# When batch 3 is folded: its copies, sending, addition and stage one in other units

## The chip, the cores and the metric

The kernel runs on one core of one Trainium2 chip. The metric is the time of one execution on the device, in microseconds; the time of a version is the median of its runs. Matrix products run on TensorE (PE in the profile), elementwise work on VectorE (DVE), ScalarE (ACT) and GpSimd (POOL). SyncE (SP) issues most of the DMA transfers; GpSimd issues some too, from its own queue.

## The reference

```python
X = np.fft.fft(x, axis=1)             # x: (8, 3072, 256), float32
X = np.fft.fft(X, axis=2)
t = X.real.astype(np.float32).reshape(24576, 256)
h = np.maximum(np.maximum(t @ w1, t @ w2), t @ w3)    # three matrices 256 x 768
out = (h @ w_out).astype(np.float32)                  # 768 x 256
```

So each of the 8 batches is mixed by a Fourier transform over 3072 rows and 256 columns, of which the real part is kept, and each of the resulting 24576 rows then goes through a layer whose hidden value is the largest of three products.

## The kernel before, in words

**What is computed where.** The transform over the 256 columns is folded into the weights once, at the start (`gE`, `gO`, `gD`, `gw`). The transform over the 3072 rows is done per batch by the class `Mix`, in two stages: seven pieces of *stage one* (`s0` to `s6`, L546), whose results ACT copies to `z_all`, and six pieces of *stage two* (`k0` to `k5`, L570 and L572, and a small `end`), whose results ACT copies to the batch's tile `t`, an even part `tE` and an odd part `tO`. Output rows come in pairs, row r and its mirror image, from even plus odd and even minus odd.

**The units.** A batch's second half, the layer, is cut into three blocks of 512 columns and six chunks of the hidden dimension: 18 units per batch. A unit makes the hidden values of its chunk for the plus rows (`unit_plus`, L590 and L591) and, one unit later, for the minus rows (`unit_minus`, L598); ACT (L604) and DVE (L605) take the largest of the three. Between them PE works off a queue of output products (`l2_block`, L615, 12 for each of four slots per block). A slot's output also needs the linear part: `l2_even` (L628, copied to `even` by ACT) and `l2_odd`, a product of the odd part into the same bank `po` (L639), of which DVE makes `other` (L642) and POOL the second half of the line `even` (L645). DVE then adds the line to `po` and gives `ot` (L665). There are two `po` banks, so the L639 of a slot waits for the L665 of the slot two before it. The plus rows of `ot` are stored by SP (L678), the minus rows by POOL with an indirect DMA (L668, the scatter; 128 KB). There are six `ot` buffers.

**Folding a batch.** While the units of batch b run, the input of later batches is made ready. For batches 2 to 7, the *folded* ones, it goes like this:

- `fetch` loads four chunks of the batch's rows, fp32, to four buffers `xs` (`load_chunk`: four DMAs of 198 or 192 KB per chunk on SP's queue, L111, and five small ones for the last chunk, L123).
- `turn_part` makes POOL copies. A *mirrored* one (L177) puts half of a chunk, turned round and in bf16, to the one tile `xb`; every second one is followed by a small copy (L181). A *natural* one (L172) puts half of a chunk to the batch's tile `xw`. There are eight of each per batch. A chunk's buffer `xs` is free for the next load when its mirrored and natural copies are done.
- `send_turned` sends `xb` to memory (`held`) with eight DMAs of 96 KB on SP's queue (L190).
- `add_turned` adds `held` to `xw` with two accumulating DMAs of 384 KB on POOL's queue (L199).
- Stage one of the batch reads `xw`.

**Who decides the order.** The order of every engine's instructions is written out by the program: `at(b, unit, fn)` puts a step behind the unit `unit` of batch b (a unit of 18 or more is one of the batch after it), and the main loop runs the steps planned for a unit when it has issued that unit. Each engine works its own instructions in this order, and one that waits holds up what is queued behind it on the same engine, DMA issues on SP's and POOL's queues among them.

During batch b, batch b + 1 goes through stage one and two (`begin`, and `steady`, units 8 to 20 in 13 steps), batch b + 2 is copied, sent and added, and the chunks of batch b + 3 are loaded (L852 to L869). Before the change, the folded batches have one plan, except that the one folded during batch 0, batch 2, has a later one.

Of the kernel before, what the change touches and what calls it, by code (L numbers as in the profile page):

```python
# [33 lines left out]
def kernel(  # L34
# [127 lines left out]
    def turn_part(b, ch, part):  # L162

        xs = raw[b, ch]
        if b not in turned:
            xw = xw_pool.tile([96, 34 * 128], BF16, name="xw", tag="xw")
            turned[b] = xw.rearrange("p (dl bb) -> p dl bb", bb=128)
        v = turned[b]
        half, natural = part % 2, part // 2
        if natural:  # L170
            d0, d1 = ((0, 17), (17, 33))[half]
            nc.gpsimd.tensor_copy(v[:, d0:d1, ch * 32:ch * 32 + 32],  # L172
                                  xs[:, 0:32 * 64].rearrange("p (bb dl) -> p dl bb", dl=64)[:, d0:d1, :])
            return
        c0 = 96 - 32 * ch
        d0, d1 = ((0, 16), (16, 32))[half]
        nc.gpsimd.tensor_copy(mir[:, d0:d1, c0:c0 + 32],  # L177
                              bass.AP(xs.tensor, xs.offset + 33 * 64 - 1 - d0,
                                      [xs.ap[0], [-1, d1 - d0], [-64, 32]]))
        if half:  # L180
            nc.gpsimd.tensor_copy(v[:, 33, c0:c0 + 32],  # L181
                                  bass.AP(xs.tensor, xs.offset + 32 * 64, [xs.ap[0], [-64, 32]]))
# [3 lines left out]
    def send_turned(b):  # L186

        hd = turn_pool.tile([8, 12 * 4096], BF16, name="held", tag="held")
        for i in range(8):
            nc.sync.dma_start(out=hd[7 - i].rearrange("(a r) -> a r", a=12),  # L190
                              in_=xb[i * 12:(i + 1) * 12])
        held[b] = hd

    def add_turned(b):

        hd = held[b]
        v = turned[b]
        for c in range(2):
            nc.gpsimd.dma_start(out=v[:, 1 + 16 * c:17 + 16 * c, :].rearrange("p dl bb -> p (dl bb)"),  # L199
                                in_=bass.AP(hd.tensor, hd.offset + 11 * 4096 + 2048 * c,  # L200
                                            [[12 * 4096, 8], [-4096, 12], [1, 2048]]),
                                accum_op=ALU.add)
# [608 lines left out]
    def at(b, unit, fn):  # L811
        plan.setdefault((b + unit // UNITS, unit % UNITS), []).append(fn)

    def piece(b, what):
        mm = mix(b)
        if what[0] == "s":
            mm.s(int(what[1:]), turned[b])
        elif what[0] == "k":
            mm.k(int(what[1]))
        else:  # L820
            mm.end()

    def fetch(b, ch):
        raw[b, ch] = load_chunk(b, ch)
# [2 lines left out]
             ("k0",), ("k1",), ("k2",), ("k3",), ("k4",), ("k5", "end"))  # L827
    begin = {0: (11, 12, 13, 13, 14, 14, 15, 16, 16, 17, 18, 19, 20),
             1: (11, 12, 12, 13, 13, 14, 14, 15, 16, 17, 18, 19, 20),
             B - 2: (8, 8, 9, 9, 10, 11, 11, 12, 13, 14, 15, 16, 17)}  # L830
    steady = tuple(range(8, 21))

# [19 lines left out]
    for b in range(B - 1):  # L852
        for i, whats in enumerate(ahead):
            for what in whats:
                at(b, begin.get(b, steady)[i], lambda b=b, what=what: piece(b + 1, what))
        if b + 2 < B:
            mirrored, natural, send_at, add_at = (
                (range(4, 12), range(12, 20), 13, 19) if b else
                ((11, 11, 12, 13, 14, 15, 16, 17), (12, 14, 16, 18, 19, 19, 20, 21), 18, 21))
            for i in range(8):  # L860
                at(b, mirrored[i], lambda b=b, i=i: turn_part(b + 2, i // 2, i % 2))
            at(b, send_at, lambda b=b: send_turned(b + 2))
            for i in range(8):
                at(b, natural[i], lambda b=b, i=i: turn_part(b + 2, i // 2, 2 + i % 2))
            at(b, add_at, lambda b=b: add_turned(b + 2))
            if b + 3 < B:
                for ch in range(4):
                    at(b, (14, 16, 18, 20)[ch] if b else (18, 19, 21, 23)[ch],
                       lambda b=b, ch=ch: fetch(b + 3, ch))  # L869

    for b in range(B):
# [77 lines left out]
```

## Time and profile before

| | |
|---|---|
| median of 3 runs | 416.75 us (414.35 to 416.84) |
| the profiled execution's own time | 415.72 us |
| span of the profile, first to last instruction | 413.6 us |
| mean granted TensorE clock | 0.990 |
| PE busy | 390.9 us, 95% of the span |
| POOL busy | 333.5 us, 81% |
| DVE busy | 309.4 us, 75% |
| ACT busy | 266.0 us, 64% |
| L668, scatter on POOL, 92 | 103.4 us, 1124 ns each |
| L645, `even` on POOL, 92 | 70.3 us, 764 ns each |
| L177, mirrored copies, 48 | 51.3 us, 1070 ns each |
| L172, natural copies, 48 | 53.0 us, 1106 ns each |
| DMA | 62.12 MB, mean 150 GB/s; 114929 of 134758 packets under 512 B |

Busy time is the time in which an engine had an instruction under way. PE's starts are exact, its ends are modelled, so a PE that is busy all the time is at its peak only if its clock is full. The profile's slices cut the span in 40 pieces of 10.3 us; a digit is the busy share in tenths. The clock of PE is a share too: 1.00 is full speed. An issue of a DMA on SP's queue that lasts long is one that SP could not hand over; when the data has landed is in the completion records of the trace, per transfer.

### The profile page before, as it was taken

To read this page: it belongs to the slowest core of one execution; us is meant where nothing else is said; L and a number is where in the kernel's file an instruction comes from. 1 tells how busy PE (TensorE), PEld (TensorE's weight loads), DVE (VectorE), ACT (ScalarE), POOL (GpSimd) and SP (SyncE) were. 2 spreads that over 40 slices of the span, in tenths; PEclk is the share of its full clock that TensorE was granted. 3 is DMA by queue.
4 is the path that set the end of the run, shared out by engine and by line. 5 is a ranking of instruction groups with operands and counts; after the bars stand their busy time and mean duration, and the time that the engine had idled before them with its cause. 6 is when DMAs were issued, how large, how long until landed. Compare 5 with 4: busy or idle time off the path is not lost.

```text
span 413.6 us, 8843 instructions
## 1 busy us (share of the span) xinstructions
PE 390.9 (95%) x2880; PEld 261.6 (63%) x2880; DVE 309.4 (75%) x556; ACT 266.0 (64%) x489; POOL 333.5 (81%) x458
## 2 busy tenths in 40 slices
PE   0999999996599999999999999999999999999996
PEld 0465677763367666666666666766667666766665
DVE  8898766784467877768876877778777777778883
ACT  6787767664176667665776577666776676655550
POOL 9599989993889999998999898998999744446641
PEclk9999999999699999999999999999999999999999
DMA  9999894487758874698477965788552722212214
GB/s 116 190 196 184 185 216 130 117 179 145 197 152 214 175 177 144 178 197 180 128 197 191 187 163 149 200 184 183 161 142 76 133 74 78 78 51 55 101 67 139
DMA packets 134758, 62.12 MB, mean 150 GB/s; under 512 B 114929, under 2 KB 130040, under 8 KB 134136
## 3 DMA queue, kind: packets, MB, share of 16 engines
q1 hardware_dynamic: 107648, 42.22, 42.0%
q0 software_dynamic: 26128, 19.02, 22.9%
q8 instruction: 22, 0.36, 0.4%
q10 hardware_dynamic: 936, 0.33, 0.3%
q14 instruction: 24, 0.20, 0.2%
HBM read 33.74 MB, written 29.88 MB: 154 GB/s over the span
## 4 chain that ended last, share of the span: by engine, by line
PE 87%; DMA 4%; POOL 3%; SPq 2%; DVE 1%; ACT 1%; issue 1%; POOLq 0%; ACTq 0%; DVEq 0%
PE po L615 29%; PE pse L590 14%; PE pse L598 14%; PE pse L591 14%; PE ps L546 3%; POOL x L111 3%; DMA xs<-in_x_dram 3%; PE ps L570 3%; PE po L639 3%; PE ps L572 3%; PE pl L628 2%; SPq L111 1%; DMA x<-in_x_dram 1%; DVE hm L605 1%; DVE ot L665 0%
## 5 line engine op out<-in xcount | busy, mean ns | idle before, releaser
L604 ACT ACTIVATE stmp<-pse 128x512 bf16<-128x512 f32 x288 | 171.0, 600 | 51.9 <-PE pse L591 37.5
L605 DVE TENSOR_TENSOR hp<-pse,stmp 128x512 bf16<-128x512 f32 x144 | 99.5, 691 | 80.6 <-ACT stmp L604 51.8
L668 POOL DMA_INDIRECT out_dram<-ot,rows_m x92 | 103.4, 1124 | 40.1 <-DVE ot L665 25.9
L590 PE MATMUL pse<-t,gE 128*128 128x512 bf16 x288 | 109.8, 381 | 0.5
L591 PE MATMUL pse<-t,gO 128*128 128x512 bf16 x288 | 109.6, 381 | 0.0
L605 DVE TENSOR_TENSOR hm<-pse,stmp 128x512 bf16<-128x512 f32 x144 | 99.2, 689 | 3.5 <-ACT stmp L604 3.3
L615 PE MATMUL po<-wout_bf,hp 128*128 128x256 bf16 x576 | 86.2, 273 | 0.0
L615 PE MATMUL po<-wout_bf,hm 128*128 128x256 bf16 x570 | 86.0, 274 | 0.0
L598 PE MATMUL pse<-t,gD 128*128 128x512 bf16 x288 | 85.9, 380 | 0.0
L645 POOL TENSOR_TENSOR even<-even,other 128x256 f32<-128x256 f32 x92 | 70.3, 764 | 14.7 <-DVE other L642 14.7
L615 PEld LDWEIGHTS <-hp 128*128 128x128 bf16 x576 | 56.3, 98 | 25.4 <-issue 10.4
L665 DVE TENSOR_TENSOR ot<-po,even 128x512 f32<-128x512 f32 x92 | 62.8, 683 | 9.0 <-POOL even L645 9.0
L615 PEld LDWEIGHTS <-hm 128*128 128x128 bf16 x576 | 56.7, 98 | 16.9
L177 POOL CAST xb<-xs 96x512 bf16<-96x512 f32 x48 | 51.3, 1070 | 10.5 <-DMA xs<-in_x_dram 9.4
L172 POOL CAST xw<-xs 96x544 bf16<-96x544 f32 (+1 forms) x48 | 53.0, 1106 | 0.0
L574 ACT CAST t<-ps 128x512 bf16<-128x512 f32 x48 | 27.9, 586 | 34.8 <-PE ps L572 34.7
L598 PEld LDWEIGHTS <-gD 128*128 128x128 bf16 x288 | 28.2, 98 | 32.6 <-issue 0.5
L551 ACT CAST z_all<-ps 128x480 bf16<-128x480 f32 x46 | 25.0, 559 | 31.4 <-PE ps L546 31.3
L642 DVE SCALAR_TENSOR_TENSOR other<-twice,po 128x256 f32<-128x256 f32 x92 | 43.8, 476 | 0.1
L591 PEld LDWEIGHTS <-gO 128*128 128x128 bf16 x288 | 28.2, 98 | 20.5 <-issue 2.3
L590 PEld LDWEIGHTS <-gE 128*128 128x128 bf16 x288 | 28.3, 98 | 19.8 <-issue 0.9
L631 ACT COPY even<-pl 128x512 f32<-128x512 f32 x46 | 27.0, 587 | 9.9 <-PE pl L628 8.3
(178 smaller groups left out, 361.1 us busy)
## 6 DMA issues: line engine op xcount, KB each, us to landing
xs<-in_x_dram SPq DMA_DIRECT2D x84, 198.0 KB
out_dram<-ot SPq DMA_DIRECT2D x90, 128.0 KB
xs<-in_x_dram SPq DMA_DIRECT2D x28, 192.0 KB
held<-xb SPq DMA_DIRECT2D x48, 96.0 KB
xw<-held POOLq DMA_DIRECT2D x12, 384.0 KB, 9.2
raw_w<-in_moe_w_dram SPq DMA_DIRECT2D x4, 384.0 KB
out_dram<-ot,rows_m POOLq DMA_INDIRECT x92, 4.0
out_dram<-ot SPq DMA_DIRECT2D x17, 64.0 KB
```

What stands on the lines that cost most here:

```text
L172: nc.gpsimd.tensor_copy(v[:, d0:d1, ch * 32:ch * 32 + 32], xs[:, 0:32 * 64].rearrange("p (bb dl) -> p dl bb", dl=64)[:, d0:d1, :])
L177: nc.gpsimd.tensor_copy(mir[:, d0:d1, c0:c0 + 32], bass.AP(xs.tensor, xs.offset + 33 * 64 - 1 - d0, [xs.ap[0], [-1, d1 - d0], [-64, 32]]))
L590: nc.tensor.matmul(pse[:, 0:n], gE[i][:, js], te, start=True, stop=False)
L591: nc.tensor.matmul(pse[:, 0:n], gO[i][:, js], to, start=False, stop=True)
L598: nc.tensor.matmul(pse, gD[i][:, js], to, start=False, stop=True, skip_group_check=True)
L604: nc.scalar.activation(out=stmp[:, 0:n], in_=pses[0][:, 0:n], func=AX.Relu)
L605: nc.vector.tensor_tensor(out=dst, in0=src3, in1=stmp[:, 0:n], op=ALU.max)
L615: nc.tensor.matmul(po, hcols(jc), wout_bf[:, jc * 256:(jc + 1) * 256], start=False, stop=(jc == NJC - 1), skip_group_check=True)
L642: nc.vector.scalar_tensor_tensor(out=other, in0=twice, scalar=po[:, 256:257], in1=po[:, 0:256], op0=ALU.mult, op1=ALU.subtract)
L645: nc.gpsimd.tensor_tensor(out=line[:, 256:512], in0=line[:, 0:256], in1=other, op=ALU.add)
L665: nc.vector.tensor_tensor(out=ot, in0=po, in1=lin, op=ALU.add)
L668: stored(nc.gpsimd.indirect_dma_start(out, bass.IndirectOffsetOnAxis(ap=rows_m[0:128 - lo, b * 12 + slot: b * 12 + slot + 1], axis=0), ot[ ...
```

## The change

Steps are moved to other units; no step is added or removed. What was the plan for all folded batches but the first is now that for all but the first two, and the batch folded during batch 1, batch 3, gets a plan of its own. Stage one and two of batch 3, during batch 2, get their own units as well.

```diff
     begin = {0: (11, 12, 13, 13, 14, 14, 15, 16, 16, 17, 18, 19, 20),
              1: (11, 12, 12, 13, 13, 14, 14, 15, 16, 17, 18, 19, 20),
+             2: (10, 11, 11, 12, 12, 13, 13, 14, 15, 16, 17, 18, 19),
              B - 2: (8, 8, 9, 9, 10, 11, 11, 12, 13, 14, 15, 16, 17)}
     steady = tuple(range(8, 21))
...
             mirrored, natural, send_at, add_at = (
-                (range(4, 12), range(12, 20), 13, 19) if b else
-                ((11, 11, 12, 13, 14, 15, 16, 17), (12, 14, 16, 18, 19, 19, 20, 21), 18, 21))
+                ((11, 11, 12, 13, 14, 15, 16, 17), (12, 14, 16, 18, 19, 19, 20, 21), 18, 21),
+                ((5, 6, 11, 12, 13, 14, 15, 16), (7, 8, 14, 15, 17, 18, 18, 19), 17, 20),
+                (range(4, 12), range(12, 20), 13, 19))[min(b, 2)]
             for i in range(8):
                 at(b, mirrored[i], lambda b=b, i=i: turn_part(b + 2, i // 2, i % 2))
             at(b, send_at, lambda b=b: send_turned(b + 2))
...
             if b + 3 < B:
                 for ch in range(4):
-                    at(b, (14, 16, 18, 20)[ch] if b else (18, 19, 21, 23)[ch],
+                    at(b, ((18, 19, 21, 23), (16, 17, 19, 20), (14, 16, 18, 20))[min(b, 2)][ch],
                        lambda b=b, ch=ch: fetch(b + 3, ch))
```

In units of batch 1, for batch 3 (chunk by chunk, two halves each): mirrored copies from 4, 5, 6, 7, 8, 9, 10, 11 to 5, 6, 11, 12, 13, 14, 15, 16; natural copies from 12 to 19 to 7, 8, 14, 15, 17, 18, 18, 19; the sends from 13 to 17; the addition from 19 to 20. The loads of batch 4's four chunks go from 14, 16, 18, 20 to 16, 17, 19, 20. In units of batch 2, batch 3's `s0` to `s6` go from 8 to 14 to 10, 11, 11, 12, 12, 13, 13, and `k0` to `k5` from 15 to 20 to 14 to 19. On SP's queue the sends now stand behind batch 4's chunk 0 and two more stores, and one store instead of two stands between the loads of chunks 2 and 3.

## The prediction

> **What bounds the kernel now.** I read the page of the profile first, its slices before its totals.
>
> ```profile
> PE   0999999996599999999999999999999999999996
> DVE  8898766784467877768876877778777777778883
> POOL 9599989993889999998999898998999744446641
> PEclk9999999999699999999999999999999999999999
> ```
>
> PE is full from slice 2 to the end except in slices 10 and 11, about 93 to 114 us, where its clock dips too. POOL, in nine tenths of nearly every slice, has a hole there as well. So a faster PE program is not on offer, and the hole is the one thing to win. PE's table of waits agrees: behind the start-up there is one releaser, `ot` of L665, twice.
>
> ```profile
> PE warm L761 <- DVE tab L338: 10.0, 1, 10.0
> PE po L639 <- DVE ot L665: 7.9, 2, 6.4
> PE ps L546 <- ACT nat L414: 0.6, 1, 0.6
> ```
>
> The timelines say where (start, length, what; in brackets the idle time before it and its releaser): PE, then DVE, then POOL, then SP's queue.
>
> ```profile
> 96.58 0.27 PE L639 MATMUL po<-gw,t 128*128 128x257 bf16 x1 [1.50 <-DVE ot L665]
> 107.85 0.38 PE L639 MATMUL po<-gw,t 128*128 128x257 bf16 x1 [6.45 <-DVE ot L665]
> ...
> 107.10 0.69 DVE L665 TENSOR_TENSOR ot<-po,even 128x512 f32<-128x512 f32 x1 [6.84 <-POOL even L645]
> ...
> 93.88 1.07 POOL L177 CAST xb<-xs 96x512 bf16<-96x512 f32 x1
> 94.88 0.24 POOL L181 CAST xw<-xs 96x32 bf16<-96x32 f32 x1
> 95.08 0.72 POOL L645 TENSOR_TENSOR even<-even,other 128x256 f32<-128x256 f32 x1
> 102.95 1.03 POOL L177 CAST xb<-xs 96x512 bf16<-96x512 f32 x1 [7.15 <-DMA xs<-in_x_dram]
> ...
> 86.18 8.65 SPq L111 DMA_DIRECT2D xs<-in_x_dram  x4
> ```
>
> The reader is to see a chain. SP issues chunk 1 of batch 3 from 86.18 to 94.83; its last completion record is at 102.80. POOL reached the mirrored copy of that chunk (placed at batch 1's unit 6) at 95.80 and stood 7.15 us. Queued behind it on POOL was `even` (L645); `ot` (L665) needs `even`; the next odd product (L639) needs the bank that `ot` empties. Then the windows, for the price (columns: PE, PEld, DVE, ACT, POOL busy, clock, DMA share, GB/s):
>
> ```profile
> 95.00:98.00 3.00, 1.50 (x13) 1.17 (x12) 2.17 (x4) 0.49 (x1) 0.80 (x2) 1.00 0.85 148
> 107.00:110.00 3.00, 2.15 (x13) 1.60 (x13) 2.28 (x4) 0.00 (x0) 2.83 (x6) 0.50 0.76 196
> 110.00:113.00 3.00, 3.00 (x17) 1.51 (x15) 1.38 (x2) 1.75 (x3) 2.26 (x5) 0.64 0.73 175
> ```
>
> After the long wait PE works at 0.50 and then 0.64: 2.15 x 0.50 + 3.00 x 0.36 = 2.2 us lost on top. The hole costs 1.50 + 6.45 + 2.2 = 10.1 us. Check: from first to first L590, batch 1 lasts 56.5 us (71.7 to 128.2) and batch 2 45.9, and both hold the same matmuls: 10.6.
>
> **The change, part by part.** It adds and removes no instruction. Batch 3's 16 POOL copies with their 4 small ones, 8 sends, 2 additions and stage one move; PE's sum stays. Time before is the profiled 415.72 us (span 413.6 and 2.1 around it), 1.0 below the median of 416.75.
>
> *The copies of chunk 0* (units 4, 5 to 5, 6; their natural ones up from 12, 13 to 7, 8). Nothing of them waits: chunk 0 was there at 89.25. Unit 4 is now empty, and a full copy with its small one (1.07 + 0.24, less overlap: 1.2) leaves POOL's queue ahead of the `even` at 95.08. It runs at 93.9, and the 1.50 us wait falls to 0.3: 1.2 gained.
>
> *The copy that waited* (chunk 1, unit 6 to 11). Down POOL's queue from there, by the rows (scatter L668 1.00 + 0.17 + 0.09, `even` 0.72, copy 1.07 or 1.10): `even` to 94.6, unit 6's copy and small copy 95.9, scatter 97.1, natural copy 98.2, `even` 98.9, scatter 100.1, natural copy 101.2, `even` 101.95, then units 9 and 10 without a copy: scatter 103.2, `even` 104.0, scatter 105.2. So POOL comes to chunk 1 at 105.2, and the row has it landed at 102.80. PE, no longer stopped, needs the `ot` of the first of these `even`s at 100.2 (its L639 would follow 100.81 + 0.60 directly, less 1.2) and gets it at 99.6; the second at 102.8, had at 102.7. Both waits are gone, 6.45, and with the idle stretch the 2.2 of clock. Three scatters of 128 KB now go out inside the loads' time; a scatter and a load share the engines, and at the 148 GB/s of the row three are 2.6 us of transfer, so chunk 1 lands between 102.8 and 105.4: cover 2.4 us, and POOL then has units of spare.
>
> *Chunks 2 and 3* (units 8 to 11 moved to 13 to 16). By the same count POOL arrives at 109.5 and 115.5; the completion records are 107.25 and 114.6, up to 2.6 later with the scatters. Waits of 0 to 1.7 us, taken from spare: `even` then ends some 3 us before its `ot` can start. I take nothing.
>
> *Two copies in units 14, 15 and 18, the addition at unit 20.* Units 12 to 20 hold 11 copies (12.0), 3 small ones (0.7), the addition's issue (2.06) and six slots of 1.98: 26.7 us of POOL. Batch 0's same nine units, with as crowded a stage one, last 26.0 (53.7 to 79.7). POOL falls 0.7 behind, 0 to 2.3 if it also waited for chunk 3. In batch 2 it then meets the one scatter per batch of 2.57 instead of 1.00 (145.06), behind which `even` has 1.13 us of spare in today's trace. Loss 0 to 1.2; I take 0.6.
>
> *SP's queue.* The sends move from 13 to 17, past two stores and chunk 0's load; behind them stand chunk 1's to 3's loads of batch 4 and the stores. They wait for POOL's last mirrored copy (about 120), take 4.0 to 4.8 to issue and land 3.4 after (79.97 to 83.33): 128. The addition comes to POOL's head at 128 to 131, so it waits for nothing, and batch 4's first mirrored copy, which overwrites `xb`, at 134. The stores held behind the sends have six `ot` buffers, nine units, some 23 us. Cost nothing; if the sends were 3 us later, POOL would stand at the addition for that time.
>
> *Batch 4's loads* move by 2, 1, 1 and 0 units (14, 16, 18, 20 to 16, 17, 19, 20), nearer the addition. Chunks 0 and 1 took 7.4 us today from first issue to last landing, chunk 2, issued 2.7 ahead of the addition, 13.3, chunk 3 13.6. The copies are at units 22 to 29, six to eight units behind, 15 to 20 us, and POOL's lag on top. Covered: nothing.
>
> *Stage one of batch 3* (units 8 to 20 now 10 to 19, three pairs). Two pairs per unit stand in batch 1 without a PE wait. The addition took 11.3 us (136.87 to 148.19), so the folded tile is there at 139 to 142; PE comes to unit 10's products at 145 (today 155.19, less 10.1). Nothing, with just under 3 us of cover.
>
> Sum: 1.2 + 6.45 + 2.2 - 0.6 = 9.2; 415.7 - 9.2 = 406.5, and by the median 407.5. I say 407.0.
>
> [...] The row first: after 1.50 us of idle the clock stayed 1.00, after 6.45 it was 0.50. [...]
>
> Second, 88 to 96 us, with the addition on queue 0:
>
> ```profile
> q0 software_dynamic: 443, 0.86, 64.5%
> q1 hardware_dynamic: 1980, 0.50, 28.8%
> ```
>
> SP's queue moved 0.50 MB in 8 us; from 80 to 86 it moved 0.86 in 6: 44% of the rate. [...] That speaks against bringing loads to the addition. By it the sum would be the next rival's, 409.5 to 411.5; by the completion records it stays 406.5.
>
> **Rivals.** *A: the hole moves to batch 4's copies.* Loads beside the addition took 13.3 to 16.6 us (86.18 to 102.80). Chunks 2 and 3 now share it with chunk 1's tail, and a landing over 20 us leaves POOL waiting 3 to 5 beyond its spare of 1.1: PE loses 3, with the clock 5. Against it: today chunk 3 goes out at 145.03 behind two stores and lands at 158.65, 0.5 ahead of its copy (159.12); now one store stands ahead of it. 406.5 + 3 to 5 = 409.5 to 411.5. *B: little changes:* POOL waits for chunk 1 at unit 11 as it did at 6. That takes a landing 6 us or more past 105.2, more than the three scatters weigh: 413 to 418. *C: slower.* Sends, addition and stage one in one row with less room: if the addition leaves POOL late, PE stops at stage one's first product. Slower than before begins where the wait and its 2.2 of clock pass the 9.2 won: a wait of 7, an addition landed after 152, issued after 140.7. Issued at 147 it would be 406.5 + 13.3 + 2.2 = 422. For it: SP's queue stood 8.65 us on one chunk. Against: today the sends land 2.5 us before the addition in the like order of batch 0. *D: the change doesn't do what it says:* excluded, the instruction order has POOL's chunk 1 copies behind unit 11.
>
> **The numbers.** Forecast 0.70 (404.5 to 409.5), A 0.14, B 0.09, C 0.07. One per cent, 4.2 us, is about what a measurement of this kernel can tell. Faster than 412.6: forecast and most of A, 0.82; within 0.11; slower 0.07. Lower end: all 10.6 won is 405.1 from the profiled run and 403.8 from the lowest (414.35), so 404.5; upper end, A's, 411.5.
>
> **What would show it.** PE's waits for `ot` under 1 us in all; the clock 1.00 to the end; POOL at chunk 1 near 105 without a long gap; batch 1 near 46 us. A gap of POOL at a mirrored copy in batch 2 is A, one at unit 11 B, a PE wait at L546 C. Wrong altogether if batch 1 is short and another batch has grown.

## The result, and the profile after

The median of the changed kernel is 410.74 us (410.5 to 411.18, 4 runs), that of the kernel before beside it 415.64 us (414.35 to 416.84, 4 runs). The ratio is 0.9884, with an interval of 0.9843 to 0.9925. The gain is 4.9 us; the forecast was 9.2. The profiled execution of after took 411.18 us, its span is 409.1 us (before 413.6), its mean clock 0.996 (before 0.990).

The slices of after (PE, POOL, PE's clock), and below them the one row of PE's table of waits behind the start-up (total us, times, longest):

```profile
PE   0999999999999979999999999999999999999996
POOL 9599999999899968989999899989999744536641
PEclk9999999999999998999999999999999999999999
```

```profile
PE po L639 <- DVE ot L665: 3.8, 3, 2.5
```

The hole in slices 10 and 11 is gone from all three rows. A smaller one stands in slices 15 and 16, about 143 to 164 us, where before had none. It has the same releaser as before. PE's timeline of after says where the three waits are:

```profile
94.91 0.27 PE L639 MATMUL po<-gw,t 128*128 128x257 bf16 x1 [0.40 <-DVE ot L665]
...
103.11 0.27 PE L639 MATMUL po<-gw,t 128*128 128x257 bf16 x1 [0.88 <-DVE ot L665]
...
152.39 0.27 PE L639 MATMUL po<-gw,t 128*128 128x257 bf16 x1 [2.49 <-DVE ot L665]
```

The first two are in batch 1 and replace waits of 1.50 and 6.45. The third is in batch 2, and its cause reads off POOL's timeline as it did before, one batch later:

```profile
104.43 1.06 POOL L177 CAST xb<-xs 96x512 bf16<-96x512 f32 x1
...
149.90 1.03 POOL L177 CAST xb<-xs 96x512 bf16<-96x512 f32 x1 [3.70 <-DMA xs<-in_x_dram]
150.90 0.71 POOL L645 TENSOR_TENSOR even<-even,other 128x256 f32<-128x256 f32 x1
```

At 104.43 POOL takes the mirrored copy of batch 3's chunk 1, for which it had stood 7.15 us, without a wait. At 149.90 it starts the first mirrored copy of batch 4's chunk 2, 3.70 us after it could have; `even` is queued behind it. The chain of waits ties this to one load (start, length, what):

```profile
132.29 6.76 SPq L111
...
139.09 10.66 DMA xs<-in_x_dram
...
150.90 0.72 POOL even L645
...
151.65 0.70 DVE ot L665
...
152.39 0.27 PE po L639
```

SP's queue shows the load among its neighbours:

```profile
125.62 4.10 SPq L111 DMA_DIRECT2D xs<-in_x_dram  x4
129.82 0.92 SPq L678 DMA_DIRECT2D out_dram<-ot  x1
130.84 11.19 SPq L111 DMA_DIRECT2D xs<-in_x_dram  x4
142.12 4.10 SPq L678 DMA_DIRECT2D out_dram<-ot  x1
146.32 4.95 SPq L111 DMA_DIRECT2D xs<-in_x_dram  x4
```

Chunk 1 goes out in 4.10 us. Chunk 2, begun at 130.84, takes SP 11.19 us, and its last completion record is at 149.75: 18.9 us from first issue to landing. POOL had issued the addition of batch 3 at 130.09, 0.75 us ahead of it. These are the addition in after (POOL's timeline) and, below it, the same chunk's issue in before (SP's queue):

```profile
130.09 2.03 POOL L199 DMA_DIRECT2D xw<-held  x2
...
134.15 4.86 SPq L111 DMA_DIRECT2D xs<-in_x_dram  x4
```

In before the chunk landed at 147.50, after 13.3 us, and POOL came to its copy at 154.96, 20.8 us after the first issue. In after POOL came at 146.20, 15.4 us after it. So the load became 5.6 us longer, and the time that it had became 5.4 us shorter.

The windows give the price (columns as in the prediction):

```profile
149.00:152.00 3.00, 0.90 (x5) 0.29 (x3) 0.35 (x1) 1.44 (x3) 2.10 (x3) 1.00 0.75 174
152.00:155.00 3.00, 2.61 (x21) 2.07 (x21) 1.92 (x4) 0.54 (x2) 1.87 (x4) 0.69 0.68 179
155.00:158.00 3.00, 3.00 (x19) 1.72 (x18) 1.22 (x2) 2.02 (x5) 2.70 (x3) 0.75 0.59 190
```

After a gap of only 2.49 us the clock was halved for one stretch, 3.41 us long in the trace's clock records, which costs 1.7 us more (3.41 x 0.5).

The batches, from first L590 to first L590, are the account:

| | batch 0 | batch 1 | batch 2 | batch 3 | batch 4 | batch 5 | batch 6 |
|---|---|---|---|---|---|---|---|
| before | 47.22 | 56.48 | 45.91 | 45.90 | 46.02 | 45.91 | 47.35 |
| after | 47.24 | 47.73 | 50.95 | 45.54 | 46.02 | 45.91 | 47.35 |

Batch 1 lost 8.75 us. Batch 2 gained 5.04, and 4.2 of it are the gap and the halved clock (2.49 + 1.7); 0.36 is stage work that moved over from batch 3. The other 0.5 has no wait of PE beside it; e7 below, whose batch 2 has no wait, is 0.4 longer than 45.91 + 0.36 as well. Of the 4.5 us between the spans, the seven batches make 4.05; most of the rest is a start-up that was 0.6 us shorter in this execution and has nothing to do with the change.

### The profile page after: what moved, and what is told of

Its sections match the earlier page's. It is cut to its first block, busy times and chain, and to the rows that moved or that the text cites. A ratio compares the mean times of both kernels' runs of the same rounds, so it can differ in the third digit from the quotient of the medians.

```text
span 409.1 us, 8839 instructions
## 1 busy us (share of the span) xinstructions
PE 390.8 (96%) x2880; PEld 261.5 (64%) x2880; DVE 309.3 (76%) x556; ACT 265.8 (65%) x489; POOL 333.6 (82%) x458
## 4 chain that ended last, share of the span: by engine, by line
PE 84%; DMA 5%; POOL 3%; SPq 2%; DVE 2%; issue 1%; ACT 1%; POOLq 0%; DVEq 0%; ACTq 0%
PE po L615 28%; PE pse L590 14%; PE pse L591 14%; PE pse L598 14%; PE ps L546 3%; DMA xs<-in_x_dram 3%; PE po L639 3%; PE ps L572 3%; PE ps L570 2%; PE pl L628 2%; SPq L111 2%; POOL x L111 2%; DMA x<-in_x_dram 1%; DMA raw_w<-in_moe_w_dram 1%; POOL out_dram L668 1%
## 5 line engine op out<-in xcount | busy, mean ns | idle before, releaser
L590 PE MATMUL pse<-t,gE 128*128 128x512 bf16 x288 | 109.8, 381 | 0.5
L590 PEld LDWEIGHTS <-gE 128*128 128x128 bf16 x288 | 28.3, 98 | 20.1 <-issue 0.9
```

What stands on the lines that cost most here:

```text
L590: nc.tensor.matmul(pse[:, 0:n], gE[i][:, js], te, start=True, stop=False)
```

## The experiments

My theory was that chunk 2's load is late because it shares the DMA engines with the addition. The rivals: it only stands too late in SP's queue; the copy asks too early; the new units of stage one make the wait; or there is too little room for SP's queue and the DMA engines at this pace, so that whatever is moved, a wait comes back elsewhere. The kernels ran on several chips, on which the kernel before took 415.6 to 418.1 us in the median, so the ratio is to before on the same chip. Of the intervals only e3's and e11's lie apart from after's; by its time none of the others can be told from it. The batch lengths are finer, but each row of them is one execution: the trace of e8 is of its shortest run (409.00 of 409.00 to 414.85 us), those of e1 and e11 are of their longest. "Waits" are PE's over 0.3 us, parted by a semicolon where the next batch begins.

| kernel | ratio to before (interval) | batch 1 | 2 | 3 | PE's waits in batches 1 to 4 |
|---|---|---|---|---|---|
| before | 1 | 56.5 | 45.9 | 45.9 | 1.50, 6.45 |
| after | 0.9884 (0.9843 to 0.9925) | 47.7 | 50.9 | 45.5 | 0.40, 0.88; 2.49 |
| e1_loads_back | 0.9865 (0.9794 to 0.9937) | 49.2 | 51.0 | 45.5 | 0.91, 1.84; 2.60 |
| e2_chunk2_at_18 | 0.9869 (0.9816 to 0.9922) | 48.9 | 49.5 | 45.6 | 0.45, 1.96; 2.66 |
| e3_loads_alone | 0.9976 (0.9931 to 1.002) | 55.5 | 45.9 | 45.9 | 1.67, 3.14, 2.25 |
| e4_stage_back | one run, 411.09 us | 48.6 | 49.1 | 45.9 | 0.41, 1.71; 1.64, 0.44, 0.59 |
| e5_eight_ot | 0.9884 (0.9812 to 0.9957) | 46.7 | 50.1 | 45.8 | 0.38; 2.82 |
| e6_loads_early | 0.9862 (0.9826 to 0.9899) | 48.3 | 48.8 | 45.5 | 0.39, 1.47; 1.17, 0.80 |
| e6b_loads_early_eight_ot | 0.9904 (0.9862 to 0.9946) | 46.7 | 52.7 | 45.5 | 0.39; 4.42 |
| e7_no_addition | one run, 408.6 us | 47.9 | 46.6 | 45.5 | 0.43, 0.97; none |
| e8_batch4_later | 0.9875 (0.983 to 0.992) | 48.6 | 47.6 | 45.5 | 0.42, 1.72; 0.37 |
| e9_batch4_later_eight_ot | 0.9849 (0.9796 to 0.9903) | 46.7 | 47.0 | 47.9 | 0.38; none; 1.43, 0.58 |
| e10_before_no_addition | one run, 411.7 us | 52.5 | 45.9 | 46.2 | 0.78, 3.24 |
| e11_batch5_later_too | 0.9808 (0.9779 to 0.9838) | 46.6 | 48.7 | 46.1 | 0.35; 1.12, 0.78; 0.40; 1.69, 0.73, 0.58 |

**The loads' units.** Three kernels change nothing but where the chunks of batch 4 are loaded: after with the old units, after with chunk 2 one unit earlier, and before with the new units.

```diff
# e1_loads_back, to after
-((18, 19, 21, 23), (16, 17, 19, 20), (14, 16, 18, 20))[min(b, 2)][ch]
+((18, 19, 21, 23), (14, 16, 18, 20), (14, 16, 18, 20))[min(b, 2)][ch]
# e2_chunk2_at_18, to after
-((18, 19, 21, 23), (16, 17, 19, 20), (14, 16, 18, 20))[min(b, 2)][ch]
+((18, 19, 21, 23), (16, 17, 18, 20), (14, 16, 18, 20))[min(b, 2)][ch]
# e3_loads_alone, to before
-(14, 16, 18, 20)[ch] if b else (18, 19, 21, 23)[ch]
+((18, 19, 21, 23), (16, 17, 19, 20), (14, 16, 18, 20))[min(b, 2)][ch]
```

> The changed kernel with batch 4's loads back at units 14, 16, 18, 20 and all else as changed. Queue theory: after the change chunk 2's load of batch 4 is handed over at 130.84, 0.75 us behind the addition (130.09), because it stands on SP's queue behind the eight sends and chunk 1's load; the addition then starves it and POOL waits 3.70 us at its copy. With chunks 0 and 1 ahead of the sends, chunk 2 goes out near 126, four us ahead of the addition, lands before 140, POOL's wait at it is gone and PE's wait of 2.49 falls to 0 to 1; batch 2 lasts 46 to 47.5 us and the time is 406 to 408. Crowding theory: loads, sends and addition fill the same stretch whatever their order, and one of chunks 2 and 3 still lands late: PE waits 2 us or more in batch 2, time 409.5 to 411.5.

> The changed kernel with the loads of batch 4 at units 16, 17, 18, 20: chunk 2 alone one unit earlier. Queue theory: it still stands behind the sends and chunk 1's load and passes one store only (0.92 us), so it goes out at 129.8 to 130, beside the addition; landing and wait stay: POOL waits 2 to 4 us at it, PE 1 to 2.5, time 409.5 to 411. Unit theory (it is one unit too late): it goes out 2.5 us earlier, POOL's wait shrinks to 1, PE's to 0 to 0.5, time 407 to 408.

> The kernel before with batch 4's loads alone at units 16, 17, 19, 20. The hole in batch 1 stays (PE waits 7.9 us in two pieces). Queue theory: the sends at unit 13 are out of the way, chunks 0 and 1 go out at about 129 and 133, chunk 2 behind the addition (about 137): it lands 17 to 19 us later and POOL waits at its copy; PE waits 1 to 3 us more in batch 2, time 417 to 420. If the loads' units are not what cost the changed kernel its 5 us in batch 2, the time is that of the kernel before, 415 to 416.5, with batch 2 at 46 us.

None of the three moves the hole away. e1's batch 2 is as long as after's, but POOL waits at another instruction, the addition (its table of waits):

```profile
POOL xw L199 <- DMA xs<-in_x_dram: 4.1, 1, 4.1
```

The sends stood behind two loads on SP's queue instead of one, went out from 127.89 to 132.87 (in after 120.89 to 125.58) and landed at 136.44, and the addition was issued at 137.06. The row names a load as the releaser, but the addition needs the sends; their records are the ones to look at. e2 moved chunk 2 past one store, but SP was so far behind that its first issue, at 131.14, is only 0.2 us ahead of the addition; it landed at 149.83, and PE's wait is 2.66. So the edit hardly tests whether an earlier load would help; it shows that a unit earlier in the plan isn't necessarily one in time. e3 shows that the later load units alone cost nothing: batch 2 lasts 45.9 there without a wait, and the ratio can't be told from 1. Its chunk 2 took 14.6 us, from 135.10 to 149.70, and had 19.2 us to POOL's copy.

**Without the addition.** e7 is after without batch 3's addition, so that part of the computation is left out; e10 is before without batch 2's addition, the one beside which before's chunk 1 of batch 3 was loaded.

```diff
# e7_no_addition, to after
+            if b != 1:
-            at(b, add_at, lambda b=b: add_turned(b + 2))
+                at(b, add_at, lambda b=b: add_turned(b + 2))
# e10_before_no_addition, to before: the same with b != 0
```

> The changed kernel without the addition of batch 3 (its two accumulating DMAs of 384 KB are left out; batch 3's rows then miss their mirrored part). If the addition is what starves chunk 2's load: it lands within 8 us of its hand-over (138 to 140), POOL does not wait at its copy, batch 2 lasts 45.9 to 46.5 us, the time is 5 us below the changed kernel, about 406. If it is SP's queue behind the sends: hand-over at 130.8 and a wait of 2 us or more at its copy stay, batch 2 at 49 to 50.5, time 409 to 410.5.

> The kernel before without the addition of batch 2 (left out in batch 0; batch 2's rows miss their mirrored part). If the addition is also what made chunk 1 of batch 3 land 16.6 us after its hand-over: it lands within 8 us (by 95), POOL does not wait 7 us at its copy, batch 1 lasts 46 to 48 instead of 56.5 us, time 8 to 10 below the kernel before. If the loads are late by SP's queue alone: the wait of 6.45 stays to more than half and batch 1 lasts over 51.

In e7 batch 2 has no wait and lasts 46.6. SP's queue in the same place, chunk 2 and chunk 3:

```profile
132.19 3.48 SPq L111 DMA_DIRECT2D xs<-in_x_dram  x4
...
137.11 3.02 SPq L111 DMA_DIRECT2D xs<-in_x_dram  x4
```

Chunk 2's issue takes 3.48 us instead of 11.19, and it has landed at 139.01, 6.8 us after its first issue instead of 18.9. The windows from 132 us, after first, then e7, show the difference (the last two columns are the DMA engines' busy share and GB/s):

```profile
132.00:138.00 6.00, 6.00 (x41) 3.78 (x40) 4.94 (x9) 3.48 (x6) 5.59 (x7) 1.00 0.86 146
```

```profile
132.00:138.00 6.00, 6.00 (x41) 3.78 (x40) 5.31 (x10) 3.23 (x6) 4.23 (x5) 1.00 0.92 224
```

The engines are about as busy in both, but with the addition they move 146 GB/s instead of 224. In these 6 us, 145 packets of 4096 bytes on POOL's queue took 63 of the 16 engines' 96 us in after, and SP's queue got 719 packets of 256 bytes through; in e7 it was 53 packets, 10 us, and 3764 packets. So chunk 2 shared the DMA engines with the addition, and without the addition there is no wait, although e7 hands the chunk over later (132.19) and leaves it less time to POOL's copy (14.2 us): a late place in SP's queue is not enough. But the sharing is not the whole delay. In after the addition had landed at 141.71, and the last two of the chunk's four DMAs had all but one of their recorded completions by 144.64 and 145.10, before POOL came at 146.20. The missing ones are at 148.81 and 149.75; as far as the records go, the 3.70 us of POOL's wait are theirs alone (last section). As I read it, the addition made the chunk late enough to meet them; in e7 it had landed long before. e10 bounds it from the other side. Without the addition, batch 3's chunk 1 lands at 92.83 instead of 102.80, and its wait of 7.15 is gone. But batch 1 falls only from 56.5 to 52.5: POOL now waits 3.44 and 3.04 us at the next two chunks (chunk 2 lands at 103.50). The addition is what made the one load late, and the loads of that batch are late behind it for more reasons than that.

**Stage one back, and eight buffers.** e4 is after without the new line of `begin`; e5 has two more `ot` buffers.

```diff
# e4_stage_back, to after
-             2: (10, 11, 11, 12, 12, 13, 13, 14, 15, 16, 17, 18, 19),
# e5_eight_ot, to after
-    out_pool = ctx.enter_context(tc.tile_pool(name="outbuf", bufs=6))
+    out_pool = ctx.enter_context(tc.tile_pool(name="outbuf", bufs=8))
```

> The changed kernel with stage one and two of batch 3 back at units 8 to 20, one step each. The addition landed at 141.7 in the changed kernel, PE would come to unit 8's products at about 140.8: a new wait of PE at L546 of 0 to 2 us, and the wait at chunk 2's copy stays (POOL 3 to 4, PE 0.5 to 2.5 less what PE already lost): batch 2 50.5 to 52, time 411 to 412.5. If the pairs of stage one in a unit cost PE something by themselves: batch 2 below 50, time 409 to 410.

> The changed kernel with eight instead of six buffers for ot. Buffer theory: the 0.88 us wait of PE at 103.11 is an addition of DVE into an ot buffer whose store, held up on SP's queue behind a load, landed only at 102.24; with eight buffers that wait is gone, and the wait of 2.49 us at 152.39 stays, since POOL stands at chunk 2's copy until 149.90: time 0.5 to 1.2 us lower than the changed kernel, 409.5 to 410.5. If the 0.88 us has another cause, nothing changes: 410.5 to 411.2. If the buffers were what makes both waits, 406 to 408.

With stage one in its old units no wait appears at L546, and batch 2 has the same kind of hole: as far as this one run tells, its new units are neither the gain nor the loss. e5 takes the wait of 0.88 out of batch 1 (46.7). In after, `even` of that slot was done at 101.29, yet DVE's `ot` started at 102.36: it wanted a buffer whose store SP had issued at 93.28, behind chunk 1's load, and which landed at 102.24. The other kernels bear it out: the second wait of batch 1 is 0.88 to 1.96 us long with the changed plan and six buffers, and in none of the four with eight. The hole of batch 2 is still there, 2.82, and here the clock did not follow (window of e5 just after it):

```profile
153.00:156.00 3.00, 2.58 (x25) 1.88 (x25) 1.96 (x4) 1.08 (x3) 1.91 (x4) 1.00 0.58 150
```

**Loads much earlier.** e6 puts chunks 0 and 1 of batch 4 six and two units earlier and chunk 2 one; e6b adds the eight buffers.

```diff
# both, to after
-((18, 19, 21, 23), (16, 17, 19, 20), (14, 16, 18, 20))[min(b, 2)][ch]
+((18, 19, 21, 23), (10, 15, 18, 20), (14, 16, 18, 20))[min(b, 2)][ch]
# e6b too
-    out_pool = ctx.enter_context(tc.tile_pool(name="outbuf", bufs=6))
+    out_pool = ctx.enter_context(tc.tile_pool(name="outbuf", bufs=8))
```

> The changed kernel with batch 4's loads at units 10, 15, 18, 20: chunk 0's buffer is free from unit 8 on, so its load goes out ahead of the crowd, chunk 1's ahead of the sends, and the sends then start no more than 1 us later than in the changed kernel (120.9). Room theory: between the last mirrored copy and the addition SP's queue and the DMA engines have room for the sends and one chunk, not for the sends and two; moving chunk 0 out makes room. Chunk 2 goes out at 126 to 127, lands before 136; no POOL wait at it; the addition goes out at 130 to 131.5; chunk 3 is the one beside the addition, with 20 us to its copy. Batch 2 lasts 46 to 47 us, batch 1 47.7 as in the changed kernel; time 4 to 5 us below the changed kernel, ratio to the kernel before 0.974 to 0.979. Crowding theory: the wait goes to chunk 3 or to the addition as it did when the loads went back to 14, 16, 18, 20: batch 2 of 49 to 51, ratio 0.986 to 0.989.

> The same with eight ot buffers. Room and buffer theory: batch 1 at 46.7 besides batch 2 at 46 to 46.5, 0.5 to 1.2 us below the run with six buffers; ratio 0.971 to 0.977. If the buffers do nothing once the loads are early: the same time as with six.

Both fall on the sends, as e1 did: they leave SP until 131.6 and 133.0 instead of 125.6, and POOL stands at the addition, in e6b longest of all:

```profile
POOL xw L199 <- DMA xs<-in_x_dram: 5.7, 1, 5.7
```

What eight buffers won in batch 1 was given back there with interest (batch 2 52.7, PE's wait 4.42). In all three kernels with earlier loads (e1, e6, e6b) the sends, and the addition behind them, came later for it.

**Copies later.** If loads can't come sooner, the copies can ask later. e8 gives batch 4 a plan between that of batch 3 and the common one; e9 adds eight buffers; e11 does the like for batch 5.

```diff
# e8_batch4_later, to after
                 ((5, 6, 11, 12, 13, 14, 15, 16), (7, 8, 14, 15, 17, 18, 18, 19), 17, 20),
-                (range(4, 12), range(12, 20), 13, 19))[min(b, 2)]
+                ((4, 5, 7, 8, 10, 11, 12, 13), (6, 9, 14, 15, 16, 17, 18, 19), 14, 19),
+                (range(4, 12), range(12, 20), 13, 19))[min(b, 3)]
# e9_batch4_later_eight_ot: e8 and bufs=8
# e11_batch5_later_too, to e9
+                ((4, 5, 6, 7, 9, 10, 12, 13), (8, 11, 14, 15, 16, 17, 18, 19), 14, 19),
-                (range(4, 12), range(12, 20), 13, 19))[min(b, 3)]
+                (range(4, 12), range(12, 20), 13, 19))[min(b, 4)]
```

> The changed kernel with a plan of its own for batch 4 as well: its mirrored copies at units 4, 5, 7, 8, 10, 11, 12, 13 of batch 2 instead of 4 to 11, natural ones at 6, 9, 14 to 19, sends at 14 instead of 13; loads, addition and stage one as they were. Deadline theory: chunk 2's load of batch 4 goes out beside the addition as before and lands at 148 to 151, but its first copy now stands two units (5 us) later, so POOL does not wait for it; what is left is a PE wait of 0 to 1.3 for an ot buffer, whose store stands behind that load. Batch 2 lasts 46 to 47.7 us, later batches 45.5 to 46, ratio to the kernel before 0.976 to 0.982. Backlog theory: DMA is simply behind by some 5 us, and what isn't waited for here is waited for at the next copies or at batch 4's stage one: batches 1 to 4 together stay at 190 us, ratio 0.986 to 0.990.

> The same with eight ot buffers. Deadline and buffer theory: no PE wait over 0.5 us in batches 1 to 3, batch 1 46.7 us, batch 2 45.9 to 46.5, ratio 0.972 to 0.978. Backlog theory: what batch 1 gains by the buffers batch 2 gives back at the addition, as in the run with early loads: same total as with six.

> The plan with batch 4's copies later and eight ot buffers, and batch 5's copies of chunk 2 one unit later and of chunk 3 two units later as well, its sends one unit later, its natural copies at units 8, 11 and 14 to 19. If the hole is a late landing against a fixed unit and only moves on (deadline theory), the waits left in that plan (POOL 1.65 and 2.49 at batch 5's mirrored copies, PE 1.43 and 0.58) go, since chunk 2 landed 193.9 against a copy ready at 192.4 (now some 195) and chunk 3 at 199.9 against 198.3 (now some 203): batch 3 46.0 instead of 47.9, the span 405 to 406, and no wait over 0.5 behind it, because each later batch's loads have a shorter queue in front of them; the ratio to the kernel before 0.980 to 0.984. If the backlog theory is the whole of it (SP's queue and the DMA engines have too little room at this rate), the wait comes back one batch further on at nearly the same size (1.5 to 2.5 us of PE in batch 3 or 4) and the span stays 407 to 408.

In e8 chunk 2 still takes SP 10.17 us and lands at 150.06, but POOL comes to its copy later and finds it there:

```profile
151.57 1.07 POOL L177 CAST xb<-xs 96x512 bf16<-96x512 f32 x1
```

Batch 2 falls to 47.6 and the span of this run, the shortest of five, to 407.1; the ratio of 0.9875 can't be told from after's 0.9884. In e9 a wait comes up one batch on, at two chunks of batch 5 (POOL's timeline):

```profile
194.04 1.07 POOL L177 CAST xb<-xs 96x512 bf16<-96x512 f32 x1 [1.65 <-DMA xs<-in_x_dram]
...
200.75 1.05 POOL L177 CAST xb<-xs 96x512 bf16<-96x512 f32 x1 [2.49 <-DMA xs<-in_x_dram]
```

e11 shrinks that (PE's 1.43 and 0.58 in batch 3 become 0.40), and three waits of 3.0 in all are there in batch 4, besides two in batch 2, the first after POOL had stood 1.52 us at the addition. POOL's timeline:

```profile
197.84 1.06 POOL L177 CAST xb<-xs 96x512 bf16<-96x512 f32 x1 [1.96 <-DMA xs<-in_x_dram]
...
243.52 1.04 POOL L177 CAST xb<-xs 96x512 bf16<-96x512 f32 x1 [2.96 <-DMA xs<-in_x_dram]
...
249.48 1.07 POOL L177 CAST xb<-xs 96x512 bf16<-96x512 f32 x1 [1.80 <-DMA xs<-in_x_dram]
```

So in these traces a later copy cures the place that it is put to, and the lateness is handed on: the part of e11's expectation that names too little room came true, the promised quiet behind it did not. Its profiled run, 412.09 us, is the longest of its six (407.54 to 412.09), so the batch lengths in the table stand for its bad end. Its median is 409.83 us beside 417.44 us of before. It is the only kernel whose interval lies wholly below after's (0.9838 against 0.9843), by a hair and on another chip; the two were not run side by side, so that it beats after is likely and not shown. e9 can't be told from after.

## Why the prediction was right or wrong

The time, 410.74 us, lay in the range only because that reached to rival A. The likeliest case, 407.0, given 0.70, was not what happened. Rival A, given 0.14, was: the hole moved to batch 4's copies, at 409.5 to 411.5. By the prediction's own sign, "Wrong altogether if batch 1 is short and another batch has grown", its main account failed: batch 1 is short and batch 2 has grown by 5.04 us. That the time lay in the range was luck for that account.

- **Copies of chunk 0:** right. The wait of 1.50 became 0.40 (0.3 expected); that slot's `even` was done at 94.14 (94.6 counted).
- **The copy that waited:** right, with both its prices. POOL came to chunk 1 at 104.43 (105.2 counted), after its landing at 101.5 (102.8 to 105.4 counted). Of 10.15 us in batch 1, 8.87 are gone (10.15 less 0.40 and 0.88), where the step expected 9.85.
- **Chunks 2 and 3 of batch 3:** right, POOL did not wait.
- **SP's queue:** right on the sends, which landed at 128.74 (128 forecast), so that the addition waited for nothing. Wrong on the buffers: "six `ot` buffers, nine units, some 23 us" was reckoned for the stores behind the sends. The store that came late stood earlier, behind chunk 1's load, where before PE was waiting anyway. It cost the 0.88, and the four kernels with eight buffers show that this was the buffer.
- **Stage one of batch 3:** right that it costs nothing (e4). POOL's lag of 0.6 us in batch 2 can't be seen apart from the hole; the 0.4 us that batch 2 of e7 is longer without any wait may be it.
- **Batch 4's loads, "Covered: nothing":** this is the step that failed. It took the landing times of 13.3 and 13.6 us that loads beside the addition had in before, and set them against 15 to 20 us of cover. Chunk 2 took 18.9. The cover was counted rightly, it was 15.4 us; the load's time was the term that was wrong, by 5.6 us. The prediction had a third row, 16.6 us for the load at the very hole of before, but used it under rival A alone and did not set it against the 15 us here. In before, the 10 us of the hole were also time in which SP's queue and the DMA engines could catch up; that this is why the loads landed sooner is my reading. What is shown: e3, which keeps the hole and moves the loads, has no wait in batch 2; e7, which keeps the moves and drops the addition, has none either. So the loss needs the addition beside chunk 2 and the rest of the change as well, which cut the cover from 20.8 us to 15.4 (19.2 in e3). With the cover of before, even 18.9 us would not have been waited for.
- **The clock:** the sum took a short wait to cost its own length. The one row of before for that, 1.50 us without a change, was too far from the gaps that came. Gaps of 2.49 (after), 2.60 (e1) and 3.24 (e10) were followed by one halved stretch, 1.7 us more, and so was the one of 4.42 (e6b) and the pair of 3.14 and 2.25 (e3); gaps of 2.66 (e2) and 2.82 (e5) were not. The mean clocks of the profiled runs agree: 0.994 to 0.996 in the first five, 1.0 in e2, and in e5 (0.998) the window after the gap has 1.00. In after the halved stretch begins at 153.11, when the gap has been over for 0.7 us. So from 2.49 to 2.82 us the length of a gap alone does not tell whether the clock drops, and no run shows what does.
- **Loads beside the addition:** the row of 88 to 96 us had SP's queue at 44% of its rate, and the prediction set this aside in favour of the completion records of before. The row was the one to follow: in e7, with only scatters on POOL's queue, the load took 6.8 us instead of 18.9.

So 9.2 expected, less 0.98 (waits of 1.28 left in batch 1 instead of 0.3), less 4.2 for the hole of batch 2 and plus the 0.6 of lag in its place, is 4.6. The batches gained 4.05; most of the 0.6 between the two is the 0.5 of batch 2's growth that has no wait beside it. B and C did not come up: POOL had no gap at unit 11, and L546 no wait.

## What to carry to other kernels

A landing time that is read beside a stall may not hold once the stall is gone: here a load grew from 13.3 to 18.9 us while its cover shrank from 20.8 to 15.4. So the covers of the next transfers have to be reckoned with the pace that the gain brings, and with the longest load on record, not the nearest. Where loads, sends and an accumulating transfer shared one stretch, each load that was moved earlier made the sends late; moving the consumer later cured its place, and a part of the lateness came back a batch later. Here a wait of 2.5 us on TensorE cost 4.2 (after), while behind one of 2.8 the clock stayed full (e5).

## What the runs showed of the hardware

**Single packets while POOL waits.** The DMA engines' busy share from 143 to 150 us of after, in 40 slices of 0.175 us, and GB/s below it; one engine of 16 alone reads 0 or 1:

```profile
DMA  9999987443621100000109999200000013579976
GB/s 181 209 234 247 268 252 252 149 133 130 184 66 60 48 25 25 25 25 25 25 25 423 364 329 335 73 25 13 18 18 19 18 35 88 135 180 230 227 179 155
```

While POOL waits from 146.2 to 149.9, and for a microsecond ahead of that, the DMA engines are nearly all idle twice, from 145.1 to 146.5 and from 147.5 to 148.7. The packets in the first stretch follow each other to within 4 ns, on POOL's queue (q0) and SP's (q1) in turn (one of 4 bytes, at 145.540, is left out):

```
start us, us, queue, bytes
145.486 0.018 q1 256
145.500 0.159 q0 4096
145.655 0.018 q1 256
145.670 0.159 q0 4096
145.825 0.018 q1 256
145.839 0.159 q0 4096
```

The records do not number the engines, but one packet at a time, on two queues in turn, reads here as one engine that takes the two queues in turn: the load's packets of 256 bytes start 0.17 us apart, against 0.014 us in the second stretch, where they run alone. The completion records agree: in the chunk's last two DMAs a single one is outstanding from 145.10 on. The chunk's last record is at 149.75, and 2.6 of the 4.6 us before it are such single packets. Why these packets come so late is open, and no run tried another spread of them. The addition had landed 3.4 us before, and in e10, without an addition there, chunk 2 of batch 3 ends the same way: its last DMA has all recorded completions but one by 100.32, the last at 103.50. One lead: once per batch a scatter takes POOL 2.6 us instead of 1.0, and in after (issued at 136.18) its last record, at 147.86, is 3.4 us behind the one before it; in before, e7 and e10 it is 3.0, 1.7 and 2.1 behind. No run was made without that scatter.

**What the accumulating transfer cost.** Among the 4096-byte packets on POOL's queue from 130 to 146 us, the median is 0.327 us in after and 0.159 in e7, where only scatters are among them; together they took 103 us of the 16 engines' time against 24. So, as an estimate, one addition of 768 KB weighs some 80 engine-us, 5 us of all sixteen. A chunk's four loads, some 3,100 packets of 256 bytes at 0.018 us (the median there), weigh 3.5.
